# A two-layer linear-attention and gated-unit kernel: the second layer's keys by seven block products in float16

## The chip, the cores and the metric

The kernel runs on one core of one Trainium2 chip. The core has TensorE (matrix products into PSUM, eight banks of 512 float32 columns in each of 128 partitions), VectorE, ScalarE and GpSimd for the rest, and queues for transfers: SP's above all, and GpSimd's. Each engine works through its instructions in order and waits on semaphores for the others. The metric is the time of one execution in microseconds (us), lower is better.

## The reference

```
x = A_x                                    # 2048 x 1024, bfloat16
x = x + A(layernorm(x))                    # linear attention, 32 heads of 32
x = x + B(layernorm(x))                    # gated bilinear unit, 1024 -> 3584 -> 1024
x = x + A(layernorm(x))                    # the same weights again
x = x + B(layernorm(x))

A(x):  q, k, v = x @ wqkv, in heads
       phi(t) = where(t > 0, t + 1, exp(t)) + 1e-6
       kv = phi(k)^T v                     # 32 x 32 a head
       z = sum over tokens of phi(k)
       o = (phi(q) kv) / (phi(q) . z + 1e-6)
       return o @ wo
B(x):  return ((x @ w_gate) * (x @ w_up)) @ w_down
```

The layers are numbered 0 to 3 in the program: A is 0 and 2, B is 1 and 3. "The second attention layer" is layer 2.

## The kernel before

The 2048 tokens are 16 tiles of 128; four tiles are a group of 512. The order on each engine is the order in which the program is written (a manual schedule): functions return lists of small steps, and the loops place these steps between the matrix products. X holds the tokens in bfloat16 (16 tiles). Normalised tiles xn_a go through transposing DMAs on SP's queue (tx, L307) into xT, four slots of one group each. A large part of the memory is eight buffers K0 to K7, reused by stage: heads (4096 columns) hold projection weights (wk in K5 and K4, wq in K6 and K7, wv in K3 and K1), tails hold phi(k) (pk) and normalised tiles.

**Attention layer** (layer_A, L686). For each token tile k_tile (L383) makes the keys, two halves of 512 columns with 8 matmuls each, into a pair of PSUM banks; the four pairs are taken in turn. phi (L351) takes the exponential on ScalarE (L357), for a split phi also x + 1 + 1e-6 (L361), then min and add (L362) and maximum (L364, or L366 straight from PSUM) on VectorE. sum_unit (L403) adds the tiles of phi(k) up for z. Then xk_pair (L390) multiplies the normalised tokens with phi(k) over all 16 tiles: eight pairs of 32 matmuls. Three of them (layer 0) or one (layer 2) stand before the query tiles, the rest between them. z_parts and z_unit turn the running sum into a row, z_column into a column; q_tile (L437) makes queries and phi(q), over_den and flush divide by the denominator a few tiles later; kv_unit, kvo_unit and out_tile finish the layer.

In layer 2 the weights wq and wv are asked for at the start (L751, L752), and the 16 key tiles carry one running sum each and the norms of the last group (norm_fill(3, 3, xn_a), L754), which run on VectorE.

**Layer 0 besides** takes the norms of the feed-forward weights: 42 pieces of 128x2048 are loaded (scan_fetch, L206; the first 14 on SP's queue, the rest on GpSimd's) and squared and summed on ScalarE (scan_step, L216). scale_sum to scale_bits (L229 to L252) make power-of-two scales of them, in three columns. Ten of the scans stand between key tiles, at every second unit from the 10th to the 28th (L745).

**Feed-forward layer** (layer_B, L842). It has two passes of 1024 tokens. Gate and up products already use seven block products where plain blocks need eight: product (L575), after (L590), with snapshots of running sums that ScalarE copies out of PSUM (L595, L598) and additions on VectorE (L543). Sums of weight blocks are made by sums (L545), sums of token blocks by t_fill (L571). The scheme holds four bank pairs, a, b and c of which change with the unit (bank, L850). The down products (down_step, L897) run in seven steps i, each of four parts j; a part is 14 matmuls. At the end of the second pass of layer 1, the norms of groups 0 and 1 are VectorE steps (fill, L981), and in step i = 6 VectorE also normalises the four tiles of group 2 (L998 to L1003). Both halves of the key weights are loaded after step 4 (L1013).

Of the kernel before, what the change touches and what calls it, by code (L numbers as in the profile page):

```python
# [14 lines left out]
I32 = mybir.dt.int32  # L15

# [21 lines left out]
def kernel(  # L38
# [12 lines left out]
    P = 128  # L51
# [70 lines left out]
    G21 = [W[:, 7 * D + i * NB:7 * D + (i + 1) * NB].bitcast(F16) for i in range(2)]  # L122
    count = {}
# [42 lines left out]
    mhalf = const.tile([P, 3], F32, tag="mhalf", name="mhalf")  # L166
# [19 lines left out]
    acc = const.tile([P, 3, NU], F32, tag="acc", name="acc")  # L186
    fac = const.tile([P, 3], F32, tag="fac", name="fac")
    kap = const.tile([P, 1], F32, tag="kap", name="kap")
    part = const.tile([P, 3], F32, tag="part", name="part")
    partb = const.tile([P, 3], BF16, tag="partb", name="partb")  # L190
# [10 lines left out]
    EARLY, MID = 26, 34  # L201
# [31 lines left out]
    def scale_pow(lo, hi):  # L233

        ps = mm_tile()
        nc.tensor.matmul(out=ps[:, lo:hi], lhsT=ones[:], rhs=partb[:, lo:hi], start=True, stop=True)
        nc.vector.tensor_scalar(out=part[:, lo:hi], in0=ps[:, lo:hi], scalar1=1e-30, scalar2=None, op0=ALU.max)

# [3 lines left out]
    def scale_bits(lo, hi):  # L242

        for m in range(lo, hi):
            nc.vector.tensor_scalar(out=fac[:, m:m + 1], in0=fac[:, m:m + 1], scalar1=(4.0, 2.0, 16384.0)[m],
                                    scalar2=None, op0=ALU.mult)
        bits = fac[:, lo:hi].bitcast(I32)
        nc.vector.tensor_scalar(out=bits, in0=bits, scalar1=0x7F800000, scalar2=None, op0=ALU.bitwise_and)
        if hi == 3:
            nc.vector.tensor_tensor(out=kap[:], in0=fac[:, 0:1], in1=fac[:, 1:2], op=ALU.mult)  # L250
            nc.vector.tensor_tensor(out=kap[:], in0=kap[:], in1=fac[:, 2:3], op=ALU.mult)
            nc.vector.reciprocal(out=kap[:], in_=kap[:])  # L252

# [136 lines left out]
    def xk_pair(c):  # L390

        def run():
            ps = mm_pair()
            n, j = divmod(2 * c, KD)
            for ts in (range(NT - 2), range(NT - 2, NT)):
                for i in range(2):
                    for t in ts:
                        nc.tensor.matmul(out=ps[:, i, :], lhsT=xn_a[t][:, (j + i) * P:(j + i + 1) * P],  # L398
                                         rhs=pk[t][:, n * NB:(n + 1) * NB], start=(t == 0), stop=(t == NT - 1))
            nc.scalar.copy(out=XK[n][:, j:j + 2, :], in_=ps)  # L400
        return run

    def sum_unit(t, eng):  # L403
# [55 lines left out]

    def over_den(t, pq):  # L460
# [9 lines left out]
    def den_sums(t, pq, den):  # L470
# [3 lines left out]
        if t % 2:  # L474
            nc.vector.tensor_scalar(out=den[:], in0=den[:], scalar1=1e-6, scalar2=None, op0=ALU.add)
            nc.vector.reciprocal(out=den[:], in_=den[:])

    def den_divide(t, pq, den):
# [4 lines left out]
        tx(pq, t, t // TPG)  # L483

# [200 lines left out]

    def layer_A(li):  # L686
        sks = [sum_unit(t, nc.vector) for t in range(1, NT)]
        first_A = li == 0

# [4 lines left out]
        if li == 0:  # L694
# [31 lines left out]
            for i, (t, n) in enumerate(units):  # L726
# [18 lines left out]
                if 10 <= i <= 28 and i % 2 == 0:  # L745
                    scans()
                if t > 10 and n == 1:
                    sks.pop(0)()
            load_qkv(wq, 0)
        else:  # L750
            load_qkv(wq, 0)  # L751
            load_qkv(wv, 2)  # L752
            count["mm"] = 5
            fill = norm_fill(3, 3, xn_a)  # L754
            for t in range(NT):
                phi(*k_tile(t), True)
                do(fill[2 * t:2 * t + 2])
                if t > 0:
                    sks.pop(0)()

        xk = [xk_pair(c) for c in range(KD)]
        first = 3 if first_A else 1
        for i in range(first):
            xk[i]()
            do(sks[5 * i:5 * i + 5])
            if i == min(2, first - 1):
                z_parts()
            scans(3 if i < 2 else 2)
        rest = xk[first:]
        XT_ = 11  # L770

        for t in range(XT_):
# [6 lines left out]
            q_tile(t, li > 0, done=2 * (t < XT_ - 1))  # L779
            do(xks)  # L780
            if t == 0:
                z_unit()
            elif t == 2:
# [8 lines left out]
            scans((1, 2, 2, 2, 2, 2, 2, 2, 1, 0, 0)[t])  # L792
# [14 lines left out]
        if first_A:  # L807
            job(9, dp[0][0])
            job(14, lambda: scale_sum(2, 3))
            job(13, dp[1][0])  # L810
            job(18, lambda: scale_pow(2, 3))
            job(20, lambda: scale_root(2, 3))
            job(22, lambda: scale_bits(2, 3))
            for i in range(1, 9):
# [241 lines left out]
```

## Time and profile before

| | |
|---|---|
| three runs | 1490.03, 1490.81, 1495.17 us; median 1490.81 |
| profiled execution | 1490.81 us, its span 1489.0 us |
| granted TensorE clock | 1.00 |
| layer 0, keys | 7 to 67 us of the span |
| layer 1, second pass | 495.4 to 749.1 us |
| layer 2, keys | 749.1 to 804.3 us |
| layer 2, key-value pairs, queries | 804.3 to 923.1 us |
| layer 2, output | 923.1 to 978.4 us |
| layer 3 | 978.4 to 1489.0 us |

PE is TensorE's matmuls, PEld its weight loads, DVE is VectorE, ACT ScalarE, POOL GpSimd, SP the transfer queue. A row of a group of instructions reads: line, engine, operation, output <- inputs, shape, count, then busy time in us and the mean of one in ns, then the idle time of the engine just before them and what ended it. A row in order of time reads: start, duration, engine, line, operation, count, and in brackets the idle time before it and its releaser. The time of a stage in a profile is one execution's.

### The profile page before, as it was taken

How to read it: one execution, taken by the hardware profiler on the slowest of the kernel's cores; microseconds unless marked ns; L12 is line 12 of the kernel's file. 1: busy time of each engine (PE TensorE's matmuls, PEld its weight loads, DVE VectorE, ACT ScalarE, POOL GpSimd, SP SyncE). 2: the span in 40 equal slices, each digit the busy share in tenths (PEclk: the TensorE clock that was granted, in tenths of full speed). 3: DMA queues.
4: the chain of work that ended last, by engine and by line, in shares of the span. 5: the costliest groups of instructions: out<-in, count | busy, mean ns of one | idle time of the engine just before them, and what ended most of it. 6: DMA issues, size and time to landing. Idle time of an engine off the chain costs nothing.

```text
span 1489.0 us, 17622 instructions
## 1 busy us (share of the span) xinstructions
PE 1482.4 (100%) x6997; PEld 675.9 (45%) x6997; DVE 1007.3 (68%) x1426; ACT 707.8 (48%) x650; POOL 89.5 (6%) x206
## 2 busy tenths in 40 slices
PE   9999999999999999999999999999999999999999
PEld 3444544444444444444444445444444444444444
DVE  7856888888774577768285457767776845777532
ACT  4977695777501455540045337545554015666200
POOL 2120121000010000001020000200000100000000
DMA  7875856776655233327470014343332753333442
GB/s 213 225 238 165 234 134 189 211 208 203 207 175 168 81 95 93 89 100 227 133 170 0 15 31 126 64 122 94 89 85 100 236 167 99 85 85 86 151 167 85
DMA packets 269650, 202.74 MB, mean 136 GB/s; under 512 B 101760, under 2 KB 256896, under 8 KB 265984
## 3 DMA queue, kind: packets, MB, share of 16 engines
q1 hardware_dynamic: 261232, 182.61, 43.1%
q0 software_dynamic: 4032, 14.68, 3.0%
q10 hardware_dynamic: 4304, 4.33, 0.9%
q8 instruction: 55, 0.90, 0.2%
q14 instruction: 27, 0.22, 0.0%
HBM read 160.43 MB, written 17.04 MB: 119 GB/s over the span
## 4 chain that ended last, share of the span: by engine, by line
PE 94%; DMA 2%; ACT 2%; DVE 1%; issue 1%; SPq 0%; POOL 0%; ACTq 0%; DVEq 0%; POOLq 0%
PE Q L578 45%; PE Q L877 23%; PE Q L374 11%; PE Q L512 7%; PE Q L398 6%; DMA K<-in_A_wqkv_dram 1%; ACT K L221 1%; ACT W L357 1%; DMA X<-in_A_x_dram 1%; PE Q L492 0%; PE Q L502 0%; DVE st L260 0%; DMA K<-in_B_w_gate_dram 0%; ACT K L287 0%; SPq L138 0%
## 5 line engine op out<-in xcount | busy, mean ns | idle before, releaser
L578 PEld LDWEIGHTS <-K 128*128 128x128 f16 x3136 | 306.8, 98 | 370.0
L578 PE MATMUL Q<-XT,K 128*128 128x512 bf16 (+1 forms) x1792 | 405.7, 379 | 0.0
L877 PE MATMUL Q<-K,K 128*128 128x512 f16 (+2 forms) x1582 | 340.4, 377 | 0.0
L578 PE MATMUL Q<-TX,K 128*128 128x512 f16 x1344 | 308.4, 379 | 0.0
L540 ACT ACTIVATE K<-K,fac 128x2048 f16<-128x2048 bf16 x112 | 224.7, 2008 | 128.0 <-DMA K<-in_B_w_gate_dram 128.0
L877 PEld LDWEIGHTS <-K 128*128 128x128 f16 x1582 | 154.2, 98 | 184.6
L543 DVE TENSOR_TENSOR K<-K 128x1024 f16<-128x1024 f16 (+1 forms) x244 | 156.9, 665 | 103.5 <-ACT K L540 101.6
L357 ACT ACTIVATE W<-Q 128x1024 bf16<-128x1024 f32 (+1 forms) x68 | 65.7, 968 | 145.6 <-PE Q L374 145.5
L543 DVE TENSOR_TENSOR W<-MX,Q 128x1024 f16<-128x1024 f32 x88 | 107.3, 1220 | 38.5 <-PE Q L578 19.6
L598 ACT COPY MX<-Q 128x1024 f32<-128x1024 f32 x60 | 60.8, 1013 | 124.1 <-PE Q L578 111.1
L374 PE MATMUL Q<-K,XT 128*128 128x512 bf16 x512 | 113.8, 379 | 1.5 <-DMA XT<-ST 0.7
L374 PE MATMUL Q<-K,K 128*128 128x512 bf16 x512 | 114.1, 379 | 0.0
L543 DVE TENSOR_TENSOR W<-W,Q 128x1024 f16<-128x1024 f32 x80 | 97.6, 1219 | 18.0 <-PE Q L578 13.6
L598 ACT COPY W<-Q 128x1024 f32<-128x1024 f32 x52 | 52.7, 1013 | 92.7 <-PE Q L578 80.0
L543 DVE TENSOR_TENSOR K<-K,K 128x512 f16<-128x512 f16 (+1 forms) x148 | 87.6, 597 | 4.2
L362 DVE TENSOR_SCALAR W<-W 128x1024 bf16<-128x1024 bf16 (+1 forms) x68 | 27.5, 405 | 83.2 <-ACT W L357 83.1
L374 PEld LDWEIGHTS <-XT 128*128 128x128 bf16 x512 | 49.4, 98 | 61.6 <-DMA XT<-ST 1.2
L374 PEld LDWEIGHTS <-K 128*128 128x128 bf16 x512 | 50.0, 98 | 59.8
L582 DVE TENSOR_TENSOR K<-W 128x512 f16<-128x512 f16 x168 | 71.4, 425 | 5.8
L221 ACT ACTIVATE K<-K 128x2048 bf16<-128x2048 bf16 x36 | 68.6, 1910 | 8.2 <-DMA K<-in_B_w_down_dram 6.5
L260 DVE BATCH_NORM_STATS2 st<-X 128x6 f32<-128x512 bf16 x104 | 65.7, 673 | 2.7 <-DMA X<-in_A_x_dram 2.7
L891 DVE SCALAR_TENSOR_TENSOR W<-Q,kap,X 128x1024 f32<-128x1024 f32 x16 | 20.5, 1284 | 66.5 <-PE Q L877 66.5
(125 smaller groups left out, 1154.8 us busy)
## 6 DMA issues: line engine op xcount, KB each, us to landing
K<-WD SPq DMA_DIRECT2D x28, 1792.0 KB, 7.3
K<-in_B_w_gate_dram SPq DMA_DIRECT2D x70, 512.0 KB, 4.1
K<-in_B_w_up_dram SPq DMA_DIRECT2D x56, 512.0 KB, 5.1
K<-in_A_wqkv_dram SPq DMA_DIRECT2D x10, 1024.0 KB, 7.9
K<-in_B_w_up_dram POOLq DMA_DIRECT2D x11, 512.0 KB, 5.5
K<-in_B_w_down_dram POOLq DMA_DIRECT2D x11, 512.0 KB, 6.6
K<-in_B_w_down_dram SPq DMA_DIRECT2D x10, 512.0 KB, 5.3
WD<-K SPq DMA_DIRECT2D x10, 512.0 KB, 3.0
```

Source lines behind the costliest of these rows:

```text
L221: nc.scalar.activation(out=scan_buf[i], in_=scan_buf[i], func=ACT.Square, accum_out=acc[:, m, c:c + 1])
L260: nc.vector.bn_stats(out=stat[t][0][:, c, :], in_=X[:, t, c * NB:(c + 1) * NB])
L357: nc.scalar.activation(out=e, in_=ps, func=ACT.Exp)
L374: nc.tensor.matmul(out=ps, lhsT=xt[:, k, tl * P:(tl + 1) * P], rhs=w[:, k, :], start=(k == 0), stop=(k == KD - 1))
L398: nc.tensor.matmul(out=ps[:, i, :], lhsT=xn_a[t][:, (j + i) * P:(j + i + 1) * P], rhs=pk[t][:, n * NB:(n + 1) * NB], start=(t == 0), stop= ...
L512: nc.tensor.matmul(out=ps[:, n, :], lhsT=xT[t // TPG][:, c, tl * P:(tl + 1) * P].bitcast(F16), rhs=KVo[c][:, n, :], start=(c == 0), stop=( ...
L540: nc.scalar.activation(out=b.bitcast(F16), in_=b, func=ACT.Copy, scale=fac[:, m:m + 1])
L543: eng.tensor_tensor(out=o, in0=a, in1=b, op=op)
L578: nc.tensor.matmul(out=pair[:, m, :], lhsT=stationary(n, p, m, k), rhs=moving[p][:, k, :], start=(p in (1, 2, 5) and k == 0), stop=(k == K ...
L582: nc.vector.tensor_tensor(out=hA[i][:, u, :], in0=gu[:, 0, :], in1=gu[:, 1, :], op=ALU.mult)
L598: nc.scalar.copy(out=snaps[u, p], in_=a)
L877: nc.tensor.matmul(out=ps_[:, lo:hi], lhsT=act[:, u, j * P:(j + 1) * P], rhs=w[:, u, lo:hi], start=(p in (1, 2, 5) and u == 0), stop=(u == ...
```

## The change

1. **Keys of layer 2.** The product of one group of tokens with the key weights is split in two along tokens (even tiles and odd tiles), along the inner dimension and along the columns. Seven products of half-size blocks take the place of eight, four groups one after another (key_stage). Inputs to four of the products are sums of token blocks (key_sums), moving operands are blocks of the weights or their differences (key_weights). The weights are turned to float16 and multiplied by a power of two k (key_convert). phi works on scaled keys: snapshots carry k(1 + 1e-6) as a bias, the exponential has the scale 1/k and a bias of ln k - 1 - 1e-6, and phi(k) times k is stored in float16 (pk2). The later 1e-6 of the denominator is multiplied by k, too.
2. **The scale k.** A fourth column for the norm of the key weights: eight squares on ScalarE in layer 0 (scan_key), after units 4 to 11 of the key tiles. The weight scans between key tiles go from ten to six (units 14 to 24), with one more in the third group after the keys, two more among the query tiles and one more among the output tiles. key_scale makes the constants.
3. **Norms.** Group 2 goes from VectorE to ScalarE (norm_act in step 6 of the last pass of layer 1). Of group 3, tiles 12 and 13 go to ScalarE and 14 and 15 stay on VectorE (key_norms), in the first two groups of the keys.
4. **Order.** One key weight half is loaded a step earlier. wq is asked for in the last group, wv after the keys. The first key-value pair begins inside the key stage, two pairs stand before the queries, and tiles 13 and 15 come last in each. The running sums start in the fourth group. z_unit and z_column come one tile later, and flush starts at query tile 2.

```diff
+    pk2 = [p.bitcast(F16) for p in pk]
+    SK = [b.bitcast(F32).rearrange("p (m s) -> p m s", s=NB)
+          for b in (K[3][:, 0:2 * D], K[3][:, 2 * D:4 * D], K[6][:, 0:2 * D], K[6][:, 2 * D:4 * D], W[:, 6 * D:8 * D])]
+    SS = [K[1][:, i * D:(i + 1) * D] ... for i in range(4)]
...
+    def scan_key(i):
+        n, h = divmod(i, 4)
+        nc.scalar.activation(out=W[:, 0:D].rearrange("p (k n) -> p k n", n=NB), in_=wk[n][:, 2 * h:2 * h + 2, :],
+                             func=ACT.Square, accum_out=acc[:, 3, i:i + 1])
...
+    def key_sums(u, which):
+        a11, a12, a21, a22 = key_blocks(u)
+        for i in which:
+            o, a, b, op = ((SS[0], a21, a22, ALU.add), (SS[1], SS[0], a11, ALU.subtract),
+                           (SS[2], a11, a21, ALU.subtract), (SS[3], a12, SS[1], ALU.subtract))[i]
+            nc.vector.tensor_tensor(out=o, in0=a, in1=b, op=op)
...
+    def key_convert(n):
+        nc.vector.tensor_scalar(out=wk[n].bitcast(F16), in0=wk[n], scalar1=fac[:, 3:4], scalar2=None, op0=ALU.mult)
...
+    def key_product(u, p, pair):
...
+        for m in range(2):
+            for k in range(KH):
+                nc.tensor.matmul(out=pair[:, m, :], lhsT=st[:, k, m, :], rhs=kmove[p][:, k, :],
+                                 start=(p in (1, 2, 5) and k == 0), stop=(k == KH - 1), skip_group_check=True)
...
+    def key_snap(u, p, bank):
+        kst[u, p] = turn("sk", SK)
+        nc.scalar.activation(out=kst[u, p], in_=bank, func=ACT.Identity, bias=kq[:, 1:2])
+    def key_add(u, b, sn, bank):
+        kst[u, b] = turn("yk", yk)
+        if sn:
+            nc.vector.tensor_tensor(out=kst[u, b], in0=kst.pop((u, sn)), in1=bank, op=ALU.add)
+        else:
+            nc.scalar.activation(out=kst[u, b], in_=bank, func=ACT.Identity, bias=kq[:, 1:2])
+    def key_exp(u, b):
...
+        nc.scalar.activation(out=e, in_=kst[u, b], func=ACT.Exp, scale=kq[:, 0:1], bias=kq[:, 3:4])
...
+    def key_max(u, b):
...
+        nc.vector.tensor_scalar(out=e, in0=e, scalar1=fac[:, 3:4], scalar2=kq[:, 2:3], op0=ALU.min, op1=ALU.add)
+        for m in range(2):
+            nc.vector.tensor_tensor(out=pk2[TPG * u + 2 * m + l][:, n * NB:(n + 1) * NB], in0=y[:, m, :],
+                                    in1=e[:, m, :], op=ALU.max)
+    def key_stage(R, fill, sks, xk):
...
+        fills(3)
+        for u in range(NG + 1):
...
+            if now:
+                key_product(u, 1, a)
+                key_snap(u, 1, a)
+            else:
+                xk[0][0]()
+            if was:
+                key_exp(u - 1, 22)
+                key_product(u - 1, 4, a_)
+                key_add(u - 1, 21, 0, a_)
+                key_exp(u - 1, 21)
+                key_max(u - 1, 22)
...
+            if now:
+                key_product(u, 2, b)
+                key_add(u, 11, 1, b)
+            if was:
+                key_max(u - 1, 21)
+                if now:
+                    key_exp(u, 11)
+                key_product(u - 1, 3, c_)
+                key_add(u - 1, 12, 6, c_)
+                if now:
+                    key_sums(u, (3,))
+                    key_max(u, 11)
+            if now:
+                key_product(u, 6, a)
+                key_snap(u, 6, a)
...
+            if was:
+                key_exp(u - 1, 12)
...
+                key_product(u, 5, c)
...
+                if u == NG - 1:
+                    load_qkv(wq, 0)
+                key_product(u, 7, a)
+                key_snap(u, 7, a)
+                if u + 1 < NG:
+                    key_sums(u + 1, (0, 1))
+                key_add(u, 22, 7, c)
...
-                if 10 <= i <= 28 and i % 2 == 0:
+                if i in SCAN_KEY:
+                    scan_key(SCAN_KEY.index(i))
+                if 14 <= i <= 24 and i % 2 == 0:
                     scans()
...
-            load_qkv(wq, 0)
+            count["mm"] = 7
+            key_stage(R, key_norms(), sks, xk)
             load_qkv(wv, 2)
...
-                        t = t1 + j
-                        ln_stats(t)
...
+                    if ps == 1 and not last:
+                        if i == 5 and j == 0:
+                            key_convert(1)
+                        if i == 6:
+                            late = [lambda: key_convert(0), lambda: key_weights(0), lambda: key_weights(1),
+                                    lambda: key_sums(0, (0, 1)), lambda: key_sums(0, (2,)), lambda: key_weights(2),
+                                    lambda: key_weights(3), lambda: key_sums(0, (3,))]
+                            do(late[(0, 5, 7, 8)[j]:(5, 7, 8, 8)[j]])
+                            do(norm2[4 * j:4 * j + 4])
```

## The prediction

> **What bounds the kernel.** I read the page's busy row and its 40 slices first, then the chain that ended last, then TensorE in order of time where the change works.
>
> ```profile
> PE 1482.4 (100%) x6997; PEld 675.9 (45%) x6997; DVE 1007.3 (68%) x1426; ACT 707.8 (48%) x650; POOL 89.5 (6%) x206
> PE   9999999999999999999999999999999999999999
> PE 94%; DMA 2%; ACT 2%; DVE 1%; issue 1%; SPq 0%; POOL 0%; ACTq 0%; DVEq 0%; POOLq 0%
> ```
>
> A busy PE row alone proves little, because the matmuls overlap (379 ns each by their rows). So I count starts. This is TensorE in order of time at the second layer's keys:
>
> ```profile
> 749.09 27.79 PE L374 MATMUL Q<-K,XT 128*128 128x512 bf16 x128
> 776.72 27.79 PE L374 MATMUL Q<-K,K 128*128 128x512 bf16 x128
> 804.34 1.46 PE L398 MATMUL Q<-K,TX 128*128 128x512 bf16 x6
> ```
>
> 256 matmuls take 804.34 - 749.09 = 55.25 us, 0.2158 us each, with no idle noted. TensorE is the limit here, so each matmul taken away is worth 0.2158 us as long as nothing arrives later than now. Its whole idle time is 1489.0 - 1482.4 = 6.6 us, and most of that is the first microsecond and the last three. What else there is lies in the first layer (same view):
>
> ```profile
> 35.70 3.63 PE L374 MATMUL Q<-K,XT 128*128 128x512 bf16 x16 [0.71 <-DMA XT<-ST]
> ...
> 73.50 0.81 PE L398 MATMUL Q<-K,K 128*128 128x512 bf16 x3 [0.29 <-DVE K L366]
> ...
> 90.00 1.89 PE L374 MATMUL Q<-K,XT 128*128 128x512 bf16 x8 [0.16 <-DMA K<-in_A_wqkv_dram]
> ```
>
> **Part 1, the products.** Keys before: 16 tiles x 2 halves x 8 = 256 matmuls. After: 4 groups x 7 products x 8 = 224. The operands are float16 and bfloat16, 512 columns; the feed-forward products at L578 mix the same types and start every 165.76 / 768 = 0.2158 us on the chain. So 32 fewer: **-6.91 us**. Here a rule speaks for less: the Trainium skill, "TensorE: Matmul & The Clock Gate", section "Back-to-back issue gap", puts a sustained stream of weight load and matmul with 512 columns at about 131 ns each. By it, the estimate is 32 x 0.131 = 4.2 us. This trace shows 215.8 ns; I take 6.91.
>
> **Part 2, what the new scheme puts on VectorE and ScalarE.** One group (512 tokens) lasts 56 x 0.2158 = 12.09 us on TensorE. Prices, from the groups of instructions by shape:
>
> ```profile
> L543 DVE TENSOR_TENSOR K<-K 128x1024 f16<-128x1024 f16 x224 | 149.2, 687 | 103.5 <-ACT K L540 101.6
> L543 DVE TENSOR_TENSOR W<-MX,Q 128x1024 f16<-128x1024 f32 x88 | 107.3, 1220 | 38.5 <-PE Q L578 19.6 <-ACT MX L598 15.4
> L582 DVE TENSOR_TENSOR K<-W 128x512 f16<-128x512 f16 x168 | 71.4, 425 | 5.8
> L361 ACT ACTIVATE W<-Q,one 128x1024 bf16<-128x1024 f32 x37 | 41.1, 1110 | 0.0
> L304 ACT ACTIVATE ST<-X,of,rs 128x1024 bf16<-128x1024 bf16 x8 | 9.8, 1230 | 0.2
> L278 DVE TENSOR_SCALAR ST<-X,mv,rstd 128x1024 bf16<-128x1024 bf16 x20 | 10.1, 529 | 0.2
> ```
>
> VectorE per group: 4 input sums at 0.687 = 2.75; 3 additions from PSUM at 1.22 = 3.66; 4 min-and-add with two pointer scalars at 0.53 = 2.12; 8 maxima of 512 columns at 0.425 = 3.40. Sum 11.9; rows overlap by some 0.09 us each (L406 runs 1.22, yet the next starts 1.14 later where nothing holds it), and 19 instructions give back up to 1.7. So it needs about 10.3 to 11.9 of 12.09 us. ScalarE: 3 snapshots and one evacuation at 1.11, 4 exponentials from SBUF with two pointers at 1.23: 9.4 us. The keys before used this (two stretches of 12.1 us):
>
> ```profile
> 761.20:773.30 12.10, 12.10 (x58) 5.49 (x57) 11.62 (x20) 6.56 (x7) 3.11 (x3) 1.00 1.20 301
> 773.30:785.40 12.10, 12.10 (x58) 5.50 (x57) 8.52 (x11) 7.66 (x8) 0.00 (x0) 1.00 0.02 4
> ```
>
> Columns: length, then PE, PEld, DVE, ACT, POOL busy. A VectorE at 11.62 of 12.1 did not hold TensorE up before either.
>
> Does it now? In order of one group (0 = its first matmul, products 1, 4 of the group before, 2, 3 of the group before, 6, 5, 7; 1.73 us each): the tight place is the snapshot after product 6, since product 7 adds into the same bank. Product 6 ends at 8.63, product 7 may start at 10.36. The snapshot queues on ScalarE behind the exponential of block 11, which waits for VectorE's addition after product 2 (5.2 to 6.4), so that exponential ends near 7.5. Snapshot 8.63 to 9.65: 0.7 us of room, and 1.1 before it, so VectorE may be 1.8 us late. The addition of block 22 ends near 2.4 of the next group, and product 3 wants its bank at 5.2. VectorE idles about 0.9 us a group. I take **0** here; the ends are 0 and about +2 us (rows without any overlap and lateness adding up over three groups).
>
> **Part 3, the seam before it.** In the last down-projection step (737.0 to 749.1) VectorE was busy 7.60 us and ScalarE not at all. Taken from VectorE: the norms of tiles 8 to 11, each two statistics at 0.67, 0.21 and 0.53, about 2.1. Added in the steps 5 and 6: two conversions of 128x4096 (half of it was 0.750 at L638; about 1.3 to 1.5 each), four weight differences of 128x2048 at 1.22, four sums at 0.687. That is some 10.5 us, with two PSUM evacuations at 1.28, in two steps of 12.1. The first of those evacuations can be about 1 us late (738.5 + 1.4 + 2.4 + 2.1 = 744.4 for 743.25). Its bank is first used by product 5, at about 754.3. Hidden; without that cover it would cost its 1 us.
>
> ScalarE takes four norms there: per tile 1.05 + 0.19, 1.13 + 0.19, 1.23, which start about every 1.04, 1.13 and 1.13 us. Tiles 10 and 11 come at 738.5, so the chain ends near 748.5. Two more means (tiles 12 and 13) stand ahead of the first snapshot: to 750.6. The snapshot is ready at 750.9 and product 6 wants its bank at 752.55: 0.65 us of room after its 1.0. Cost 0; up to +1.5 if the GpSimd steps between come late. A rule speaks against this chain: "SBUF — State Buffer", section "SBUF: two separate sides", has GpSimd and a VectorE instruction that uses the shared port pair lock each other out for a whole instruction. By it, three GpSimd steps after each variance could each wait one VectorE instruction of 1.2: an estimate of +3.6 us. The rows of the same chain before: 0.55 to 0.97 us for the power step (L300) and about 0.2 for the others (L299, L301), at most 0.4 lost. I take the rows; ScalarE's next tile covers 1.1 of it.
>
> **Part 4, DMAs and waits.** The second key-weight half loads one step earlier (hidden: 12 us more than before). The query weights now wait on SP behind the last readers of the snapshots and exponentials, about 787 and 797, and take some 8 us each (7.9 is the page's median): there at 805 to 807, wanted at about 814.7 (797.5 + 28 matmuls + two products + 36 matmuls). The value weights follow, wanted at the kv product, 898 before. Transposes of tiles 8 to 15 (3.2 us to land) are sent two groups ahead of their sums. The 15 running sums at 1.22 now come late: 13 of them after the keys, to about 826. Behind them ScalarE's copy of z and the first query tile's exponential wait; its bank is wanted again by z_unit's matmuls, which stand after two key-value pairs and two query tiles, about 835. Hidden.
>
> **Part 5, the first layer.** ScalarE gets 8 squares of 128x1024 at about 1.04 (from L294) and loses 4 scans at 1.9 + 0.19 there; its idle from 28 to 39 us, 1.75 + 1.28 + 1.64, takes most of the early ones. Walking its queue I get tile 7 released at 48.5 (tile 11 wants the bank at 49.5), tile 10 at 59.5 (59.9), tile 11 at 63.0 (63.3): nothing stops, with 0.3 us to spare. The last scan now comes before tile 14, so tile 15's keys are done about 0.4 earlier: the 0.29 goes. SP is free of its last scan load some 4 to 5 us earlier than 73.57, so the query weights come earlier: the 0.16 goes. Next to be late there is tile 11's bank. Net **-0.45**, ends -1.2 (the 0.71 too) and +1.5. The four scans put off fit later (ScalarE 67.42 of 96.0 us between 90 and 186). Six tiny factor instructions (about 0.15 each) lie beside the output tiles.
>
> **Sum.** -6.91 - 0.45 = -7.36 us. The profiled execution took 1490.81 us (span 1489.0 and 1.81 around it), and it is the median of the runs too: **1483.4 us**, span about 1481.6.
>
> **The rivals.** 0.5% of 1490.8 is 7.45 us, about what a measurement of this kernel can tell from no change; my sum lies on that line.
> - A, as summed, 0.68 with -6.2 to -8.1 us (1482.7 to 1484.6): about 0.45 of it beyond the line, because the rest of the small first-layer waits may go too, 0.23 short of it.
> - B, a new wait replaces part of the gain (seam snapshot, snapshot 6, or a first-layer bank): 1 to 6 us given back, 1484.6 to 1490. For it: room of 0.3 to 0.7 us in each. Against: four pairs of banks. 0.18.
> - C, VectorE becomes the bound of the key groups. Should the new sums, min-and-adds and maxima, on strided pieces and mixed 16-bit types, run at one element a cycle (nearest row L406, 1.22 for 1024; 0.692 for 512 at L366), a group costs 2.1 + 2.1 + 2.8 more: about 17.2 after overlap, 5.1 over TensorE's time. Over three and a half groups, less 1.8 of room: +16 us, **1499**. It decides from about 16.4 us a group. Against: L543 at TX from XT takes mixed types at 1.22 for 2048. 0.12.
> - D, the products run no faster in total because mixed types slow them: 1490. L578 speaks against it. 0.02.
>
> Range 1482 to 1489: A, and B but its end. Faster 0.45, same 0.23 + 0.18 + 0.02 = 0.43, slower 0.12.
>
> **What would show it.** Right: 224 matmuls in 48.4 us with no idle noted; VectorE 10.5 to 12 us a group. Wrong: TensorE idle released by ScalarE's snapshot (B) or by VectorE (C); a first-layer idle over 0.5 us; products starting further apart than 0.216 us.

## The result, and the profile after

| | before | changed |
|---|---|---|
| median of 4 runs each, on one chip | 1490.63 us (1490.03 to 1495.17) | 1485.79 us (1485.19 to 1486.08) |
| profiled execution, its span | 1490.81 us, 1489.0 | 1486.08 us, 1484.3 |
| granted TensorE clock | 1.00 | 1.00 |

The ratio is 0.996, with a 95% interval from 0.9941 to 0.998. The change gains 4.84 us in the medians and 4.7 us of span. That is less than the 7.45 us that the prediction took as the line, though the interval lies below 1 as a whole. It is 2.4 us short of the forecast of 1483.4 us, and inside its range. The busy row of the changed kernel's page (engine, busy time, share of the span, instructions):

```profile
PE 1475.9 (99%) x6965; PEld 672.7 (45%) x6965; DVE 1030.0 (69%) x1460; ACT 739.6 (50%) x696; POOL 96.5 (6%) x219
```

The reader is to see 32 matmuls fewer (6997 before), 23 us more of VectorE and 32 us more of ScalarE. TensorE's busy time fell by 6.5 us, and its idle time went from 6.6 us to 1484.3 - 1475.9 = 8.4 us: part of the gain is lost in new waits. Where they stand follows from the first row of TensorE in each stage (times in the span):

| | before | changed | difference of the stage |
|---|---|---|---|
| layer 0, start of the first key-value pair | 66.79 | 68.19 | +1.40 |
| layer 1 begins | 241.45 | 243.03 | +0.18 |
| layer 2, keys begin | 749.09 | 750.66 | -0.01 |
| layer 2, output begins | 922.94 | 918.34 | -6.17 |
| end of the span | 1489.0 | 1484.3 | -0.10 |

So two stages count: layer 0, which loses 1.58 us, and layer 2 from its keys to its output, which gains 6.17 us where 6.91 were to be had. TensorE of the changed kernel in order of time there (start, duration, operation, count, in brackets the idle time ahead and what released it):

```profile
35.60 3.63 PE L404 MATMUL Q<-K,XT 128*128 128x512 bf16 x16 [0.57 <-DMA XT<-ST]
...
57.52 10.83 PE L404 MATMUL Q<-K,K 128*128 128x512 bf16 x48 [1.03 <-DMA K<-K]
...
170.48 1.89 PE L404 MATMUL Q<-K,K 128*128 128x512 bf16 x8 [0.78 <-DVE W L396]
...
750.66 3.62 PE L551 MATMUL Q<-K,XT 128*128 128x512 f16 x16
754.85 3.61 PE L551 MATMUL Q<-W,K 128*128 128x512 f16 x16 [0.57 <-ACT K L558]
758.30 1.89 PE L551 MATMUL Q<-K,K 128*128 128x512 f16 x8
...
782.47 3.62 PE L551 MATMUL Q<-K,K 128*128 128x512 f16 x16
```

There are three new waits in brackets: for a transposed tile at 57.52, for VectorE in the queries at 170.48, and for ScalarE's snapshot (L558) at 754.85. A fourth, of 0.3 us, hides in the 48 matmuls from 57.52 (they take 10.67 us where 48 x 0.2158 is 10.36): TensorE waits at 64.6 for the tile that was sent at 60.84 and took 3.8 us to land. The snapshot's wait is the only one in the new products. Its bracket says 0.57 us, but it costs more: 16 matmuls from 750.66 would let the next start at 750.66 + 16 x 0.2158 = 754.11, and it starts at 754.85, 0.74 us late. The bracket counts from the modelled end of the last matmul, which lies 0.16 us behind the start of the next in an unbroken stream. The 0.74 us is what the stage misses of 6.91. The two small waits of before, 0.29 and 0.16, are gone.

The four stretches of 12.09 us from the start of the new products (length, then busy time of PE, PEld, DVE, ACT, POOL, clock, DMA share, GB/s):

```profile
750.66:762.75 12.09, 11.52 (x54) 5.16 (x53) 9.03 (x14) 10.03 (x14) 3.38 (x9) 1.00 0.28 43
762.75:774.84 12.09, 12.09 (x58) 5.46 (x56) 10.74 (x21) 11.23 (x11) 1.43 (x3) 1.00 0.12 22
774.84:786.93 12.09, 12.09 (x58) 5.49 (x56) 11.67 (x21) 9.59 (x9) 0.00 (x0) 1.00 0.34 66
786.93:799.00 12.07, 12.07 (x58) 5.49 (x56) 11.14 (x20) 8.39 (x8) 0.00 (x0) 1.00 0.35 111
```

VectorE (third busy value) fills 10.7 to 11.7 of 12.09 us in the last three stretches, inside the forecast 10.3 to 11.9, and TensorE loses nothing after the first stretch.

**The seam.** What was the snapshot waiting for? ScalarE of the changed kernel in order of time:

```profile
748.12 1.24 ACT L334 ACTIVATE K<-X,of,rs 128x1024 bf16<-128x1024 bf16 x1 [0.17 <-POOL of L331]
750.48 1.24 ACT L334 ACTIVATE K<-X,of,rs 128x1024 bf16<-128x1024 bf16 x1 [1.12 <-POOL of L331]
...
753.70 1.09 ACT L558 ACTIVATE K<-Q,kq 128x1024 f32<-128x1024 f32 x1
```

The norm of tile 11 waits 1.12 us for GpSimd and ends at 751.72. Two means stand behind it, and only then the snapshot. GpSimd in the same time:

```profile
745.87 0.19 POOL L329 TENSOR_SCALAR va<-ss 128x1 f32<-128x1 f32 x1
746.14 0.57 POOL L330 TENSOR_TENSOR rs<-va,mhalf 128x1 f32<-128x1 f32 x1
746.79 1.30 POOL L331 TENSOR_TENSOR of<-nm,rs 128x1 f32<-128x1 f32 x1
748.17 1.05 POOL L329 TENSOR_SCALAR va<-ss 128x1 f32<-128x1 f32 x1
749.30 0.88 POOL L330 TENSOR_TENSOR rs<-va,mhalf 128x1 f32<-128x1 f32 x1
750.25 0.19 POOL L331 TENSOR_TENSOR of<-nm,rs 128x1 f32<-128x1 f32 x1
```

and VectorE:

```profile
745.62 1.27 DVE L1079 SCALAR_TENSOR_TENSOR X<-Q,kap,X 128x1024 bf16<-128x1024 f32 x1
746.82 1.21 DVE L544 TENSOR_TENSOR K<-K 128x2048 f16<-128x2048 f16 x1
747.95 1.22 DVE L544 TENSOR_TENSOR W<-K,W 128x2048 f16<-128x2048 f16 x1
749.09 0.68 DVE L534 TENSOR_TENSOR K<-XT,K 128x1024 f16<-128x1024 bf16 x1
```

One number for each partition takes GpSimd 0.19 us when VectorE is quiet (the last row), and 1.30 or 1.05 us beside the differences of weight blocks (L544): these steps end 0.1 us or less behind a VectorE instruction. Beside L1079, which has one of its two large inputs in PSUM (Q), the steps at 745.87 and 746.14 take no longer than alone (0.19 and 0.57). So not every VectorE instruction stretches them.

**The first layer.** VectorE, ScalarE and SP's queue of the changed kernel on the way to the transposed tile (tile 13) that TensorE waits for until 57.5:

```profile
46.90 0.43 DVE L392 TENSOR_SCALAR W<-W 128x1024 bf16<-128x1024 bf16 x1 [0.92 <-ACT W L387]
...
48.58 1.28 DVE L290 BATCH_NORM_STATS2 st<-X 128x6 f32<-128x512 bf16 x2
49.95 0.21 DVE L294 BATCH_NORM_AGGREGATE mv<-st 128x2 f32<-128x12 f32 x1
```

```profile
44.82 1.05 ACT L281 ACTIVATE W<-K 128x1024 bf16<-128x1024 bf16 x1
...
45.86 1.01 ACT L387 ACTIVATE W<-Q 128x1024 bf16<-128x1024 f32 x1
...
51.58 1.24 ACT L317 ACTIVATE K<-X,off,rstd 128x1024 bf16<-128x1024 bf16 x1
```

```profile
51.56 0.37 SPq L223 DMA_DIRECT2D K<-in_B_w_gate_dram  x1
52.84 1.24 SPq L340 DMA_TRANSPOSE K<-K  x1
```

The last of the eight squares (L281) stands on ScalarE ahead of phi's exponential (L387). VectorE waits 0.92 us for that exponential, and its statistics for tile 13 stand behind. GpSimd, the norm (L317) and the transposing DMA follow one another. ScalarE's own queue was no earlier: a scan ends on it at 51.5, just ahead of the norm. In the kernel before, the same two steps stood 1.13 us earlier, in views of ScalarE and of SP's queue:

```profile
50.45 1.24 ACT L287 ACTIVATE K<-X,off,rstd 128x1024 bf16<-128x1024 bf16 x1
```

```profile
49.07 0.57 SPq L213 DMA_DIRECT2D K<-in_B_w_gate_dram  x1
51.71 1.24 SPq L310 DMA_TRANSPOSE K<-K  x1
```

There it had 56.4 - 51.71 = 4.7 us to land before TensorE wanted it, and took 3.8; now 56.3 - 52.84 = 3.5 us are left, and it took 4.6. By these figures there are two causes. Sent 1.1 us late, a tile that lands in 3.8 us would have been 0.3 us late; landing in 4.6 us but sent in time, it would have been in time. Together they cost 1.2.

The longer landing goes with the moved scans. The fifth weight load can be sent only when the first scan has freed its buffer. With the first scan after unit 10 the loads stand behind the transposes on SP's queue, and the last one is 2.6 us old when tile 13 is sent. With the first scan after unit 14 (49.54 to 51.5 here) a load goes out at 51.56, 1.3 us ahead of the transpose. In the eight profiles with the scans of the change tile 13 lands in 3.9 to 4.6 us, tile 14 in 3.6 to 4.1 and tile 15 in 3.8 to 4.0; in the five with the scans from unit 10 (the kernel before and four of the experiments) in 3.8, 3.1 to 3.2 and 3.1. That the load slows the transpose is an inference from this split; no run moved a load alone.

### The profile page after: what moved, and what is told of

It is laid out like the page before. It is cut to its first block, busy times and chain, and to the rows that moved or that the text cites. A ratio compares the mean times of both kernels' runs of the same rounds, so it can differ in the third digit from the quotient of the medians.

```text
span 1484.3 us, 17639 instructions
## 1 busy us (share of the span) xinstructions
PE 1475.9 (99%) x6965; PEld 672.7 (45%) x6965; DVE 1030.0 (69%) x1460; ACT 739.6 (50%) x696; POOL 96.5 (6%) x219
## 4 chain that ended last, share of the span: by engine, by line
PE 87%; POOL 1%; ACT 0%; DVE 0%; issue 0%
PE Q L755 46%; PE Q L1065 22%; PE Q L689 7%; PE Q L404 5%; PE Q L430 4%; PE Q L551 3%; PE Q L679 0%; PE Q L669 0%; POOL va L329 0%; ACT K L324 0%; POOL rs L330 0%; POOL nm L325 0%; POOL of L331 0%; DVE X L1079 0%; DVE W L396 0%
## 5 line engine op out<-in xcount | busy, mean ns | idle before, releaser
L775 ACT COPY MX<-Q 128x1024 f32<-128x1024 f32 x60 | 60.8, 1012 | 124.1 <-PE Q L755 111.1
L404 PE MATMUL Q<-K,K 128*128 128x512 bf16 x384 | 86.8, 379 | 1.9 <-DMA K<-K 1.0
L404 PE MATMUL Q<-K,XT 128*128 128x512 bf16 x384 | 85.7, 379 | 1.2 <-DMA XT<-ST 0.6
L392 DVE TENSOR_SCALAR W<-W 128x1024 bf16<-128x1024 bf16 (+1 forms) x52 | 20.5, 393 | 66.7 <-ACT W L387 66.6
L1079 DVE SCALAR_TENSOR_TENSOR W<-Q,kap,X 128x1024 f32<-128x1024 f32 x16 | 20.5, 1284 | 66.1 <-PE Q L1065 66.1
L772 ACT COPY MX<-Q 128x1024 f32<-128x1024 f32 x28 | 28.3, 1009 | 71.9 <-PE Q L755 71.9
L387 ACT ACTIVATE W<-Q 128x1024 bf16<-128x1024 f32 (+1 forms) x52 | 49.2, 950 | 29.3 <-PE Q L404 29.3
L290 DVE BATCH_NORM_STATS2 st<-X 128x6 f32<-128x512 bf16 x92 | 58.2, 673 | 2.6 <-DMA X<-in_A_x_dram 2.6
L404 PEld LDWEIGHTS <-K 128*128 128x128 bf16 x384 | 37.2, 98 | 47.4 <-DMA K<-K 2.6
```

Of the source, the lines that this page charges most:

```text
L290: nc.vector.bn_stats(out=stat[t][0][:, c, :], in_=X[:, t, c * NB:(c + 1) * NB])
L387: nc.scalar.activation(out=e, in_=ps, func=ACT.Exp)
L404: nc.tensor.matmul(out=ps, lhsT=xt[:, k, tl * P:(tl + 1) * P], rhs=w[:, k, :], start=(k == 0), stop=(k == KD - 1))
L775: nc.scalar.copy(out=snaps[u, p], in_=a)
```

## The experiments

Ten kernels with an edit, each made to the changed kernel, and one run of the changed kernel again. "Keys to output" is the time from the start of layer 2's keys to that of its output, 173.85 us before and 167.68 changed. 166.94 would be the whole 6.91. Times of layer 0 are set against the one profile of the kernel before.

**The squares for the key weights' norm left out.** The norm's column is a constant, and the ten scans between key tiles are back.

```diff
...
-                if i in SCAN_KEY:
-                    scan_key(SCAN_KEY.index(i))
-                if 14 <= i <= 24 and i % 2 == 0:
+                if 10 <= i <= 28 and i % 2 == 0:
...
-            scans(3)
+            scans(3 if i < 2 else 2)
...
-            scans((2, 2, 2, 2, 2, 2, 2, 2, 2, 0, 0)[t])
+            scans((1, 2, 2, 2, 2, 2, 2, 2, 1, 0, 0)[t])
...
-            for i in range(1, 10):
+            for i in range(1, 9):
```

> Left out: the eight squares of the key weights in layer 0 (their norm is a constant here, so the scale of the keys is another one); the weight scans stand where they stood before the change. Theory L (the first layer pays about 1.6 us for the squares and the moved scans, by three waits of TensorE): layer 1 starts at 241.6 us of the span again instead of 243.2, the waits of 1.03 us (a transposed tile) and 0.78 us (a bank behind VectorE) are gone, 0.29 and 0.16 are back, time about 1484.2. Rival R (these waits come from the transfers' own scatter, not from the edit): layer 1 starts at 243 and the time stays at 1485.8.

1484.7 us median of 8 runs, ratio 0.9958 (0.9943 to 0.9972); keys to output 167.68 as before the edit. TensorE of this run (the trace lacks 3 of the 128 matmuls of the first row):

```profile
39.10 27.64 PE L404 MATMUL Q<-K,K 128*128 128x512 bf16 x125
...
74.13 0.81 PE L430 MATMUL Q<-K,K 128*128 128x512 bf16 x3 [0.92 <-DVE K L396]
```

The wait at 57.52 is gone: the first key-value pair starts at 66.79, as in the kernel before. So the late tile comes from the squares and the moved scans together; the run takes both back and does not part them. The wait for tile 15's phi is back, with 0.92 us in place of 0.29. The profiled execution itself took 1490.47 us, because the queries stopped for 3.83 us at 162.72, behind a scan that had waited 5.20 us for its data; the other seven runs lie between 1484.12 and 1485.69. So a late weight transfer can reach TensorE through a scan, but seldom does in this kernel.

**The squares late**, after units 21 to 28 of the key tiles instead of 4 to 11, with the six scans at units 10 to 20.

```diff
-    SCAN_KEY = tuple(range(4, 12))
+    SCAN_KEY = tuple(range(21, 29))
...
-                if 14 <= i <= 24 and i % 2 == 0:
+                if 10 <= i <= 20 and i % 2 == 0:
```

> The squares stay, but stand at units 21 to 28 of the key tiles, after the last norm, and the six scans at units 10 to 20, as in the kernel before. Theory L: the loop from phi to statistics to norm to transposing DMA has its old times again, the wait of 1.03 us goes and the one of 0.78 (among the query tiles) stays; time about 1484.7. Rival R2 (eight squares cost their wait wherever they stand, as ScalarE has no room in this stage): a wait of about 1 us comes back at a later tile or at the first key-value pairs, time 1485.5 to 1486.5.

1487.95 us median of 10, ratio 0.9978 (0.9969 to 0.9988): slower than the changed kernel by 2.2, and above both expectations. The first pair starts at 66.65, so no tile is late. But ScalarE is late at the last tile: with a norm and a scan it needs 3.9 to 4.1 us from one exponential to the next, over the 3.45 us that a tile takes TensorE, and then with two squares 3.13 (66.90 to 70.03), so that it hardly catches up. In the kernel before it needs 2.8 there, with one scan (62.23 to 65.02). TensorE of this run:

```profile
76.00 0.81 PE L430 MATMUL Q<-K,K 128*128 128x512 bf16 x3 [2.64 <-DVE K L396]
```

The wait of before for tile 15's phi, 0.29, is back as 2.64. So all eight squares late are no way out either.

**One pair of scans fewer in the queries.**

```diff
...
-            scans((2, 2, 2, 2, 2, 2, 2, 2, 2, 0, 0)[t])
+            scans((2, 2, 2, 2, 2, 2, 2, 2, 1, 0, 0)[t])
...
-            for i in range(1, 10):
+            for i in range(1, 11):
```

> One scan fewer at query tile 8 of layer 0, one more among the output tiles. Theory L: the exponential of query tile 9 no longer waits behind a scan that itself waits 1.5 us for its data, so the wait of 0.78 us at the first kv-output products goes: layer 1 starts at about 242.4, time about 1485.0. Rival (the eighth output tile's scan or VectorE's divisions hold the bank instead): the wait stays at 0.6 to 0.8 us, or moves to the output tiles.

1485.78 us median of 5, ratio 0.9964 (0.9951 to 0.9977). The 0.78 at 170.48 is gone. In the changed kernel the second scan at query tile 8 waited 1.50 us for its data, ahead of the next tile's exponential:

```profile
161.04 1.91 ACT L231 ACTIVATE K<-K 128x2048 bf16<-128x2048 bf16 x1 [1.50 <-DMA K<-in_B_w_down_dram]
```

One execution alone would not show that this scan is the cause, because the stop comes and goes without an edit. But it goes with the scan's wait. Six profiles have the changed kernel's layer 0: where the scan waited 1.58 and 1.50 us, TensorE stopped for 1.01 and 0.78; where it waited 0.91, 0.91, 0.81 and 0.63, for 0.24 once and else not. Nothing is won in the median. In this execution the transposes gave waits of 0.94, 0.80 and 0.29 us, and a new one of 0.35 stands at the start of layer 1. Layer 0's small waits differ from execution to execution by as much as the edit moves.

**The means behind the first snapshot.**

```diff
-        fills(3)
         for u in range(NG + 1):
...
                 key_snap(u, 1, a)
+                if u == 0:
+                    fills(3)
```

> The means of tiles 12 and 13 on ScalarE (and one VectorE statistic) are issued behind the first snapshot of the key stage instead of ahead of it. Theory S (the seam's wait is the snapshot queued behind two means, themselves behind a norm that was late): snapshot from about 751.7 to 752.7, the wait of 0.57 us goes, the key stage takes 6.9 us less than the keys before, time about 1485.1. Rival (the next bank is late then: the snapshot after product 6 behind the means): a wait of 0.3 us or more at product 7.

Keys to output is 166.95 us: the whole 6.91 less a hundredth, and no wait is left in the products. The snapshot now waits for TensorE itself:

```profile
753.18 1.11 ACT L558 ACTIVATE K<-Q,kq 128x1024 f32<-128x1024 f32 x1 [0.87 <-PE Q L551]
```

GpSimd's steps are as long as before (L331 1.29, L329 1.05). So the wait was the two means in ScalarE's queue behind a late norm. The median of 6 is 1486.0 us all the same where 1485.1 was expected, ratio 0.9964 (0.9952 to 0.9977): the profiled execution has five waits in layer 0, 0.65, 0.17, 0.54, 0.16 and 1.09 us.

**No differences of weight blocks.** VectorE's four L544 are left out; zeros, set a step earlier, stand in three of their places.

```diff
-  late = [..., lambda: key_weights(0), lambda: key_weights(1), ..., lambda: key_weights(2), lambda: key_weights(3), ...]
+  late = [..., lambda: None, lambda: None, ..., lambda: None, lambda: None, ...]
```

> Left out: the four differences of weight blocks in the last down-projection step (zeros stand in three of their places, so the keys are not the reference's); all other work stays. Theory P (GpSimd's small steps in the norm chain are held up by VectorE's instructions with two inputs in SBUF, one whole instruction each): with 4.9 us less of these, GpSimd's steps between 741 and 750 us fall from 0.9 to 1.3 us to 0.2 to 0.6, the last norm of ScalarE ends near 749 instead of 751.6, and the wait of 0.57 us is gone. Rival Q (ScalarE's own passes fill the time, GpSimd is only noted as the last releaser): the last norm still ends after 750.5 and the wait stays at 0.4 to 0.6.

One run: 1484.62 us; keys to output 166.95. GpSimd of this run, the same steps of tile 11:

```profile
747.28 0.19 POOL L329 TENSOR_SCALAR va<-ss 128x1 f32<-128x1 f32 x1 [0.63 <-ACT K L328]
747.55 0.55 POOL L330 TENSOR_TENSOR rs<-va,mhalf 128x1 f32<-128x1 f32 x1
748.18 0.19 POOL L331 TENSOR_TENSOR of<-nm,rs 128x1 f32<-128x1 f32 x1
```

The three steps now end 1.2 us behind ScalarE's squares (at 747.20) instead of 2.5 us (747.94 to 750.44). ScalarE no longer waits for them, ends its norms at 749.6, and takes the snapshot at 751.84 as soon as the product is done. Two power steps (0.88 and 1.09 us) and one step of a mean (0.60) stand beside VectorE's sums of token blocks, the rest are short. So it is VectorE's instructions with both inputs in SBUF that stretch GpSimd's steps beside them.

**Group 2's norms back on VectorE.**

```diff
-                norm2 = norm_act(2, 2, xn_a, TPG)
+                norm2 = norm_act(2, 2, xn_a, 0)
```

> Group 2's norms go back to VectorE, all else as changed. The prediction's sum gives VectorE 8.6 us more in the last step, to some 20 us in the 12.1 us of that step and what of the step before is free after 738.8: it comes to the keys about 7 us late, so the addition after product 2 and with it everything behind comes late; TensorE waits 2 to 5 us in the first group, time 1487 to 1491. Rival (VectorE's room in the first group, which has only half the work, takes it up): under 1 us of wait, time about 1485.5.

One run: 1490.39 us; keys to output 171.95, which is 5.00 over the stream without a wait. TensorE of this run:

```profile
764.35 2.43 PE L551 MATMUL Q<-W,XT 128*128 128x512 f16 x8 [2.93 <-ACT K L558]
766.57 3.08 PE L551 MATMUL Q<-K,XT 128*128 128x512 f16 x8
```

The move to ScalarE is needed. With the norms VectorE makes its addition for block 11 only at 759.71, ScalarE's exponential follows at 760.92 and, behind one more pass, the snapshot that TensorE waits for at 763.20: a stop of 2.93 us. The two rows show something else: eight matmuls take 1.73 us from start to start elsewhere, and here 2.22 and 2.91 (769.48 - 766.57). The granted clock (last column but two) in stretches of the same run:

```profile
765.00:768.00 3.00, 3.00 (x10) 1.19 (x9) 2.29 (x4) 3.00 (x5) 2.30 (x5) 0.59 0.00 0
768.00:771.00 3.00, 3.00 (x14) 1.20 (x13) 2.29 (x5) 1.93 (x3) 0.00 (x0) 0.84 0.00 0
```

Behind the stop the clock is 0.59 and 0.84 in two stretches of 3 us, and the two rows cost another 0.49 + 1.18 = 1.67 us.

**More VectorE in each group.** One addition of 1.22 us made twice, and, in a second kernel, three instructions more.

```diff
-            nc.vector.tensor_tensor(out=kst[u, b], in0=kst.pop((u, sn)), in1=bank, op=ALU.add)
+            for _ in range(2 if b == 11 else 1):
+                nc.vector.tensor_tensor(out=kst[u, b], in0=kst[u, sn], in1=bank, op=ALU.add)
+            kst.pop((u, sn))
```

In the second the count is 3 for block 11, 2 for block 22.

> Each group's first addition from PSUM is made twice: 1.22 us more of VectorE in each group of 12.09 us. By the prediction's count (about 0.9 us idle a group and 1.8 us of lateness allowed at the snapshot after product 6) TensorE waits 0 to 0.5 us more. Rival (VectorE is already at its limit, 11.9 us by the rows): about 1 us a group, 3 us in all.

> Two more copies of the first addition and one more of the last, 3.66 us more of VectorE in each group: some 14.2 us for 12.09. By the prediction's count lateness of about 2 us a group adds up, 1.8 us of it is free, so TensorE waits 3 to 6 us in the key stage in all, released by ScalarE's snapshot after product 6 or by VectorE. Rival (the banks give more room than counted): under 1 us.

With one addition: 1488.13 us, keys to output 170.23, +2.55 over the changed kernel. With three: 1495.97 us and 178.19, +10.51 where 3 to 6 were expected; 1.7 of it is a slow clock (last section). Both are one run. TensorE of the first, and ScalarE ahead of its wait:

```profile
783.63 3.61 PE L551 MATMUL Q<-K,K 128*128 128x512 f16 x16 [1.13 <-ACT K L558]
```

```profile
781.34 1.24 ACT L571 ACTIVATE K<-MX,kq 128x1024 bf16<-128x1024 f16 x1 [1.52 <-DVE MX L564]
782.49 1.09 ACT L558 ACTIVATE K<-Q,kq 128x1024 f32<-128x1024 f32 x1
```

The place is the one that the prediction named: the snapshot after product 6 queues behind the exponential of block 11, which waits for VectorE's addition. But it gives way earlier than thought: 1.22 us more in a group were to be taken up by 1.8 us of room, and they cost 2.55 us over the groups. The changed kernel's trace shows how much room there is. ScalarE, and TensorE's product 7, in the third group:

```profile
779.33 1.24 ACT L569 ACTIVATE K<-MX,kq 128x1024 bf16<-128x1024 f16 x1 [0.27 <-DVE MX L563]
780.95 1.11 ACT L558 ACTIVATE K<-Q,kq 128x1024 f32<-128x1024 f32 x1 [0.38 <-PE Q L551]
```

ScalarE is free 0.38 us before product 6 ends, and the snapshot ends at 782.06, 0.41 us ahead of product 7 at 782.47: 0.8 us, and 0.9 to 1.15 us in the groups beside it.

**The changed kernel again**, beside the next two.

> The changed kernel once more, nothing edited, beside the next one. If the first layer's waits are the edit's own (theory L), layer 1 starts near 243.0 us of the span again, with over 1 us of waits between tiles 8 and 15 of the keys; if they are scatter of the transfers (rival R), the start lies anywhere from 241.5 to 244. The key stage of layer 2 waits 0.57 us at its third product either way, and the time is 1485.8 within 0.5.

1486.0 us median of 6 (1485.53 to 1486.69), ratio 0.9964 (0.9951 to 0.9976); keys to output 167.68 again. In the first layer the transposes gave 0.67 and 0.61 us of waits where the first profile had 1.03, and the first pair starts at 68.37. In the six profiles with the changed kernel's layer 0, layer 1 begins 0.8 to 1.6 us later than before; the first one, with 1.58, is at the upper end.

**Mended, first try:** squares in two halves, four early and four late, the means behind the snapshot, one scan between the keys and the key-value pairs, and the sums for z later.

```diff
...
-    SCAN_KEY = tuple(range(4, 12))
+    SCAN_KEY = (4, 5, 6, 7, 21, 23, 25, 27)
...
-                if 14 <= i <= 24 and i % 2 == 0:
+                if 10 <= i <= 20 and i % 2 == 0:
                     scans()
-                if 8 < t < 13 and n == 1:
+                if t > 10 and n == 1:
                     sks.pop(0)()
             load_qkv(wq, 0)
+            scans()
...
-            scans((2, 2, 2, 2, 2, 2, 2, 2, 2, 0, 0)[t])
+            scans((2, 2, 2, 2, 2, 2, 2, 2, 1, 0, 0)[t])
```

> Four squares stay at units 4 to 7, where ScalarE waited for statistics before, four stand alone behind the exponentials of tiles 11 to 14; the scans are at units 10 to 20 as in the kernel before, one more comes after the last exponential, one fewer at query tile 8; the running sums stand where they stood before the change; the two means are behind the first snapshot. By theories L and S the first layer has no new wait (layer 1 starts at 241.0 to 241.7 us) and the keys of layer 2 cost 6.9 us less than before: 1.6 and 0.7 less than the changed kernel, 1483.5. Rival R2 (the squares cost a wait wherever they stand): layer 1 starts after 242.5, time 1484.7 or more.

1490.76 us median of 12 (1487.86 to 1493.96), ratio 0.9992 (0.9979 to 1.0004): the gain is gone. Keys to output is 166.94, so layer 2 is mended. Layer 0 ends 8.3 us later than in the changed kernel, with stops of 1.94 and 4.58 us behind VectorE's phi, and that behind ScalarE, and one of 0.89 behind VectorE's step for the scales (L241); three scans waited 4.87, 2.22 and 3.22 us for their weights. Which of the edits starts this was not taken apart.

**Mended, second try:** as the first, but the sums and the counts in the queries are those of the changed kernel, and the key tiles' scans end at unit 18.

```diff
...
-    SCAN_KEY = tuple(range(4, 12))
+    SCAN_KEY = (4, 5, 6, 7, 21, 23, 25, 27)
...
-                if 14 <= i <= 24 and i % 2 == 0:
+                if 10 <= i <= 18 and i % 2 == 0:
...
             load_qkv(wq, 0)
+            scans()
```

> As e11, but no scan stands ahead of the exponential of tile 12, the running sums stay at tiles 9 to 12, and the scans among the query tiles are those of the changed kernel. What e11 lost was 1.94 us because VectorE came late to tile 12 and had a sum to make for each tile after it, and 4.6 us because scans among the queries waited for their data. Theory L: the keys' first-layer waits (1.0 to 1.3 us) are gone and layer 1 starts at 241.2 to 242.2 us; with the seam's 0.7 us the time is 1484.2. Rival R3 (the scans' data, whose loads follow the scans' places, decide the first layer): a wait of over 1 us among the query tiles, layer 1 after 243, time above 1485.5.

1484.37 us median of 5 (1484.15 to 1485.55), the kernel before beside it 1490.65; ratio 0.9956 (0.9942 to 0.9971). It is the quickest of all, 1.4 and 1.6 us under the changed kernel's two medians; one of its five runs lies among the changed kernel's. TensorE of this run:

```profile
36.00 3.63 PE L404 MATMUL Q<-K,XT 128*128 128x512 bf16 x16 [1.00 <-DMA XT<-ST]
...
169.49 1.89 PE L404 MATMUL Q<-K,K 128*128 128x512 bf16 x8 [0.76 <-DVE W L396]
...
749.67 3.62 PE L551 MATMUL Q<-K,XT 128*128 128x512 f16 x16
...
794.57 1.46 PE L430 MATMUL Q<-K,TX 128*128 128x512 f16 x6
```

No tile from the 8th to the 15th is noted as late and no product waits: 208 matmuls in 794.57 - 749.67 = 44.90 us, 0.2159 each. What is left, 1.00 and 0.76, are the first layer's old wait for its second group, here longer than the 0.71 of before, and the queries' wait for VectorE. Tile 13 is sent at 52.63, only 0.2 us earlier than in the changed kernel, but the last load is again 2.6 us old, it lands in 3.8 us, and TensorE wants it 0.4 us later because of the longer wait for the second group.

## Why the prediction was right, and where it was not

The time fell inside the range, 2.4 us from the forecast. The case that came true is a mild B, not A, the likeliest. Two of the five parts failed, and the range held because it was wide enough for them: it took in up to 6 us given back. In the span, 1484.3 us against the forecast 1481.6, new waits took back 2.7 us: 0.74 at the seam and 2.03 in layer 0 (+1.58 where -0.45 was forecast), with 0.1 found elsewhere.

- **Part 1, the products: right.** Without the seam's wait, keys to output fell by 6.90 us (173.85 to 166.94 or 166.95, in four kernels). The row's 0.2158 us per matmul holds for mixed types; the rule's estimate of 4.2 us is refuted here, and so is D.
- **Part 2, the key groups: the value of 0 right, the room too large.** The prices came as taken from the rows: sums 0.684, additions 1.214, min-and-add 0.544, maxima 0.422 us. C is refuted: sums of mixed types take 0.684 us and strided maxima 0.422, no more than the rows with equal types. (C's 2.8 us for the maxima is 2.1 by its own rows, 8 x (0.692 - 0.425), so that C stood for about 1497.) But 1.22 us more of VectorE cost 2.55 us where 1.8 us of room was counted. That wait was forecast in its place; its distance was not. The term that was off is "that exponential ends near 7.5": it ends 8.1 to 8.5 us into its group, and 0.8 to 1.15 us of room are left.
- **Part 3, the seam: this step failed**, "I take the rows; ScalarE's next tile covers 1.1 of it". The rows of the chain before, with at most 0.4 us lost, come from stages where the four weight differences of 1.22 us did not exist. The chain of norms ended at 751.72; counted from the start of the keys the forecast was 748.5 - 749.1 + 750.66 = 750.1. So it was 1.6 us late for 0.65 us of room, and TensorE paid 0.74. Of the 1.6, the last tile's three steps make 1.3: they take 2.50 us behind ScalarE's squares, and 1.17 without the differences. The Trainium skill's rule named there ("SBUF — State Buffer", section "SBUF: two separate sides") was the nearer guide to the single step: 1.30 and 1.05 us each beside VectorE's two-input instructions, 0.19 without. Its sum of +3.6 us was too high, since the three steps of one tile met one long and one short instruction, and ScalarE's other tiles hid the rest. The stretching is shown by leaving the differences out, the two means in the way by moving them.
- **Part 4, transfers and waits: right.** After the first two products nothing waits up to the output, and moving the means alone brought back all of the 6.91.
- **Part 5, the first layer: this step failed**, "nothing stops, with 0.3 us to spare". The walk went along ScalarE's queue to the PSUM banks alone, and no bank stopped anything. It left out the chain of phi, the statistics, GpSimd's step, the norm and the transposing DMA: ScalarE late by 1.1 us is a transpose late by 1.1 us. It also looked at the moved scans' last load alone and not at the first, which now goes out ahead of tile 13; that tile lands in 4.6 us where it took 3.8. Forecast were -0.45 us with ends of -1.2 and +1.5; measured are +1.58, +1.02 in the second profile of the same kernel and +0.58 in the mended one. The 0.29 and 0.16 went as forecast, and 0.78 in the queries came, for which no step had looked: two scans a query tile, of which the second can wait for its data. A stop there came in three of the six profiles with this layer 0.

What stays open: layer 0's waits differ from execution to execution by 0.5 us or more, and no run has the squares without the moved scans or the scans without the squares, so that their shares are not told apart; why the first mended kernel loses 8 us there is argued from its waits for weights, not shown.

## What to carry to other kernels

When work moves onto an engine, follow every loop that passes through its queue, up to the transfer at the end, and not only the buffers that it frees; a chain with tenths of a microsecond to spare can be late by the scatter of one transfer. When loads move, look at what they now stand in front of on the same queue. A row for a tiny instruction on GpSimd is good for the company in which it was measured: look at what VectorE does beside it after the change. And of a mean, a norm or a scan that nobody waits for, ask first what stands behind it in the queue: moving three small steps past one snapshot was worth 0.7 us of the stage.

## What the hardware showed

- **A stop of 3 us costs more than itself.** Behind stops of 2.64 and 2.73 us the clock stayed at 1.00; behind those of 2.93, 3.22, 3.83 and 4.58 us it was 0.59, 0.53, 0.50 and 0.50 in a stretch of 3 us that begins within 0.7 us of the stop's end. The Trainium skill, "TensorE: Matmul & The Clock Gate", Part 1, has the clock halved after an idle window of about 3.4 us that runs free; here 2.93 us was enough. In the kernel with three more instructions on VectorE a stop of 2.73 and one of 3.22 us stand in one view of TensorE:

```profile
772.93 3.61 PE L551 MATMUL Q<-K,K 128*128 128x512 f16 x16 [2.73 <-ACT W L558]
...
788.87 5.30 PE L551 MATMUL Q<-K,K 128*128 128x512 f16 x16 [3.22 <-ACT K L558]
```

  Sixteen matmuls take 3.61 us behind the shorter and 5.30 behind the longer.
- **GpSimd's smallest steps** take 0.19 us alone, and up to 1.30 us beside a VectorE instruction of 1.2 us with both inputs in SBUF. With four such in 8 us (741.29 to 749.17), the last norm chain lost 1.3 us.
- **A transposing transfer landed later with a weight load just ahead of it** on the same queue: 3.8 to 4.0 us with the load 1.3 us ahead in eight profiles, 3.1 us with it 2.6 to 2.8 us ahead in five (tile 15). The kernels of the two sets differ in more than the load.
